# A fused attention and FFN kernel on one Trainium2 core: the last 128-token tile's output in two PSUM tiles, one for each half of the columns

## The chip, the core and the metric

The kernel runs on one core of one Trainium2 chip. The metric is the device time of one execution in microseconds (us); the median of three runs is used, and the profile is of one further execution. The engines are named as the profile names them: PE is the matrix engine (PEld its weight loads), DVE the vector engine, ACT the scalar engine, POOL the general one, SP the engine that issues most DMAs. A name with a q, SPq or ACTq, is the queue of instructions of that engine.

## The reference, cut to what matters

```python
a = exp(phi - max(phi, 2));  a = a / (sum(a, 2) + 1e-09)          # 8 batches, 8 heads, 576 tokens, 32 memories
k_m = einsum('bhsm,bhsd->bhmd', a, k);  v_m = einsum('bhsm,bhsd->bhmd', a, v)
attn = softmax(q @ k_m.T / sqrt(64))                              # per head, 576 x 32
x = (attn @ v_m), heads side by side                              # 4608 tokens x 512
h = x @ w_in                                                      # 512 -> 2048
out = maximum(0.01 * h, h) @ w_out                                # 2048 -> 512, float32
```

The change touches only the last product, `g @ w_out`, for the last 128 of the 4608 tokens, and the way from its result to DRAM.

## The kernel before, in words

The order of the work on every engine is written out by hand: two long strings, OPENING and LATER, name steps one after the other, and each step's function issues its instructions to the engines when its name comes up. No scheduler changes that order. On each engine the instructions run in the order of the strings, and an instruction waits until what it needs has been done elsewhere.

Tokens are worked in groups. Groups 0 to 2 (384 tokens each) cover batches 0 and 1, groups 3 to 16 cover the other six batches with 256 tokens each, except group 16, the last, which has 128. The hidden width of 2048 is cut into four quarters (j), and a quarter into four slices of 128 (i). Steps of the late groups are numbered by k = 4 * (group - 3) + j, so that 52 to 55 are the four quarters of group 16. For each of them the LATER string has:

- `p` (up_late, L1215): the up products of one slice into a PSUM tile `ph`, on PE (L1229);
- `v` (leaky_late): scale and leaky ReLU from `ph` to SBUF, on ACT (L1245);
- `c` and `l`: the values split into a high and a low half-precision part, ACT (L1270) and DVE (L1274);
- `d`: the down products. For the groups of 256 tokens they are down_late (L1297, 256 columns wide, with sums of weights prepared beforehand). For group 16 they are down_tile (L1324 to L1335): per slice three matmuls (high by high, high by low, low by high) of 128 x 128 by 128 x 512 that all add up in one PSUM tile `po`, 4 quarters x 4 slices x 3 = 48 in all;
- `x` and `z` for the groups of 256 tokens: the parts added up on DVE, the result scaled on ACT (L1321) and stored.

The string ends with `end`, that is `store(16, 0, ..., last=True)` (L1166): ACT scales the left 256 columns of `po` into SBUF (`obs`, L1170), DVE the right 256 (L1171), and `send` (L1156) then stores the 128 tokens in four DMAs of 32 tokens, each 32 rows of 512 floats (64 KB). Two are issued by SP and two by ACT (L1164). Every other store of the kernel goes through SP. A store's rows lie 18 rows apart in DRAM, because token 18 * x + j of a batch stands in column 32 * j + x of the tile: one store is one j and its 32 values of x.

At the end of the program SP waits for the stores that are still on their way (L1480), and a few synchronisation instructions on all engines close the span.

Of the kernel before, what the change touches and what calls it, by code (L numbers as in the profile page):

```python
# [9 lines left out]
F32 = mybir.dt.float32  # L10
# [6 lines left out]
AF = mybir.ActivationFunctionType  # L17
# [155 lines left out]
c51.0 s51 p52.0 p52.1 v52.0 d50.0 v52.1 l51.0 c51.1 d50.1 d50.2 c52.0 l51.1 p52.2 d50.3 v52.2 l52.0  # L173
d50.4 p52.3 d50.5 v52.3 d50.6 c52.1 l52.1 p53.0 p53.1 v53.0 d51.0 v53.1 d51.1 x15.p c53.0 d51.2
l53.0 p53.2 x15.0 d51.3 v53.2 d51.4 x15.1 p53.3 x15.2 d51.5 v53.3 d51.6 c53.1 p54.0 x15.3 v54.0
l53.1 d52.0 z15.0 z15.1 p54.1 d52.1 v54.1 p54.2 c54.0 d52.2 v54.2 l54.0 p54.3 d52.3 v54.3 p55.0
c54.1 d53.0 l54.1 v55.0 p55.1 d53.1 v55.1 p55.2 c55.0 d53.2 l55.0 v55.2 p55.3 d53.3 v55.3 d54.0
c55.1 l55.1 d54.1 d54.2 d54.3 d55.0 d55.1 d55.2 d55.3 end
"""


# [1 line left out]
def kernel(  # L183
# [41 lines left out]
    nc = tc.nc  # L225
    B, H, S, D = q.shape
    M = phi.shape[3]
    F = w_in.shape[1]
    E = w_out.shape[1]
    P = 128  # L230
# [8 lines left out]
    NQ = 4  # L239
    FQ = F // NQ  # L240
    NC = H * D // P
    NF = FQ // P
# [6 lines left out]
    EH = E // 2  # L249
    JT = S // 32  # L250
    JA = JT - 2
    G2 = 3
# [11 lines left out]
    ps_o = ctx.enter_context(tc.tile_pool(name="ps_o", bufs=3, space=PSUM))  # L264
# [13 lines left out]
    wi_s, wo_s = (  # L278
        [t.bitcast(F16).rearrange("p (i x) -> p i x", i=2) for t in ts[:NQ]] for ts in (wi, wo)
    )  # L280
# [26 lines left out]
    obs = const.tile([P, 3 * E], F32, name="obs")  # L307
# [777 lines left out]
    def blocks(G):  # L1085

        return [(G // 3 * 2 + x // NB, x % NB) for x in range(G % 3 * 2, G % 3 * 2 + 2)]
# [49 lines left out]
    def columns(G, t):  # L1137

        if G < G2:
            for x in range(t * P, (t + 1) * P, 32):  # L1140
                b, tb = blocks(G)[x // SB]
                yield b, tb * SB + x % SB
        else:
            x0 = 2 * S + (G - G2) * 2 * HT + t * P
            for x in range(x0, x0 + P, 32):
                yield x // S, x % S

    def row_scale(G, t):
        bs = [b for b, _ in columns(G, t)]
        if G == 0:  # L1150
            return 1.0 / WT
        if bs[0] == bs[-1]:
            return osc[:, bs[0]:bs[0] + 1]
        return osc_t[:, bs[0] // 2:bs[0] // 2 + 1]

    def send(G, t, ob, last=False):  # L1156
        for y, (b, x) in enumerate(columns(G, t)):
            rows, eng = out[b * S:(b + 1) * S, :], nc.scalar if last and y % 2 else nc.sync
            if b < FB:
                rows = rows.rearrange("(tb x j) e -> tb j x e", tb=NB, j=NJ)  # L1160
                rows = rows[x // SB, x % SB // 32]
            else:
                rows = rows.rearrange("(x j) e -> j x e", j=JT)[x // 32]
            eng.dma_start(rows, ob[32 * y:32 * y + 32])  # L1164

    def store(G, t, po, last=False):  # L1166
        so = row_scale(G, t)
        ob = obs[:, t * E:(t + 1) * E]
        if last:
            nc.scalar.activation(ob[:, 0:EH], po[:, 0:EH], AF.Copy, scale=so)  # L1170
            nc.vector.tensor_scalar_mul(ob[:, EH:], po[:, EH:], so)  # L1171
        else:
            nc.scalar.activation(ob, po, AF.Copy, scale=so)
        send(G, t, ob, last)

    pos = {}

# [30 lines left out]
    def whole(G):  # L1208

        return 2 * S + (G - G2 + 1) * 2 * HT <= B * S  # L1210
# [4 lines left out]
    def up_late(k, i):  # L1215

        G, j = G2 + k // NQ, k % NQ
        if not banks:
            banks["p1"], banks["ph"] = [ps_h.tile([P, E], F32, name="ph") for _ in range(2)]
        ph = banks["ph"][:, i % 2 * EH:(i % 2 + 1) * EH]  # L1220
        fs = slice(i * P, (i + 1) * P)
        for b, c0, n, t0 in parts(G):
            w, a = w16(b, j), a_columns(b)
            seq = [
                (halves(w, g)[:, x, fs], a[:, y, g, c0:c0 + n])
                for g in range(NG) for x, y in ((0, 0), (1, 0), (0, 1))
            ]
            for m, (lhs, rhs) in enumerate(seq):
                nc.tensor.matmul(  # L1229
                    ph[:, t0:t0 + n], lhs, rhs, start=(m == 0), stop=(m == len(seq) - 1)  # L1230
                )

    def leaky_late(k, i):
        G, j = G2 + k // NQ, k % NQ
        ph = banks["ph"][:, i % 2 * EH:(i % 2 + 1) * EH]
        st = late.setdefault(k, {})
        if "gf" not in st:
            st["gf"] = wi[NQ][:, k % 2 * 1024:(k % 2 + 1) * 1024]
            st["g"] = at(TMP + k % 3 * 7168, 7168).bitcast(F16)
        if whole(G):  # L1240
            dst = st["gf"].rearrange("p (s u x) -> p s u x", s=4, u=2)
            dst, ph = dst[:, i % 2 * 2:i % 2 * 2 + 2, i // 2], ph.rearrange("p (t x) -> p t x", t=2)
        else:
            dst, ph = st["gf"][:, i * HT:(i + 1) * HT], ph[:, 0:HT]
        nc.scalar.activation(dst, ph, AF.Prelu, scale=g_sc2[:, j:j + 1], alpha=SLOPE)  # L1245
# [13 lines left out]
    def add_g(k):  # L1259
        gf = late[k]["gf"].rearrange("p (s x) -> p s x", s=4)  # L1260
        gt = operands(k)[1]
        for x, y, z, op in (
            (0, gf[:, 0], gf[:, 2], ALU.add), (3, gf[:, 1], gf[:, 0], ALU.subtract),
            (1, gf[:, 1], gt[:, 0], ALU.subtract), (2, gf[:, 3], gt[:, 1], ALU.add),
        ):
            nc.vector.tensor_tensor(gt[:, x], y, z, op)  # L1266

    def hi_g(k, h):
        src, dst = operands(k)[h], operands(k)[2 + h]
        nc.scalar.copy(dst[:, 0], src)  # L1270

    def lo_g(k, h):
        src, dst = operands(k)[h], operands(k)[2 + h]
        nc.vector.tensor_tensor(dst[:, 1], src, dst[:, 0], ALU.subtract)  # L1274
# [44 lines left out]
    def finish(G, t):  # L1319
        ob = obs[:, (1 - t) * E:(2 - t) * E]  # L1320
        nc.scalar.activation(ob, ob, AF.Copy, scale=row_scale(G, t))  # L1321
        send(G, t, ob)

    def down_tile(k, i):  # L1324

        G, j = G2 + k // NQ, k % NQ
        if (j, i) == (0, 0):
            pos[G] = [ps_o.tile([P, E], F32, name="po")]
        g = late[k]["g"][:, 0:2 * FQ].rearrange("p (i s x) -> p i s x", i=2, s=NF)
        for m, (x, y) in enumerate(((0, 0), (0, 1), (1, 0))):  # L1330
            nc.tensor.matmul(  # L1331
                pos[G][0], g[:, x, i], wo_s[j][:, y, i * E:(i + 1) * E],
                start=(j == 0 and i == 0 and m == 0),
                stop=(j == NQ - 1 and i == NF - 1 and m == 2),
            )  # L1335
# [5 lines left out]
    steps = {}  # L1341
# [76 lines left out]
    for G in range(G2):  # L1418
        for t in range(NT):
            steps[f"Z{G}.{t}"] = lambda G=G, t=t: store(G, t, pos[G][t])  # L1420
# [4 lines left out]
    for m in range(nq):  # L1425
        for i in range(NF):
            steps[f"p{m}.{i}"] = lambda k=m, i=i: up_late(k, i)
            steps[f"v{m}.{i}"] = lambda k=m, i=i: leaky_late(k, i)
        steps[f"s{m}"] = lambda k=m: add_g(k)
        for h in range(2):  # L1430
            steps[f"c{m}.{h}"] = lambda k=m, h=h: hi_g(k, h)
            steps[f"l{m}.{h}"] = lambda k=m, h=h: lo_g(k, h)
        for n in range(7 if whole(G2 + m // NQ) else NF):
            steps[f"d{m}.{n}"] = lambda k=m, n=n: (
                down_late if whole(G2 + k // NQ) else down_tile
            )(k, n)
    for G in range(G2, G2 + NG2):
        for n in ("1", 0, 1, 2, 3):
            steps[f"x{G}.{'p' if n == '1' else n}"] = lambda G=G, n=n: combine(G, n)
        for t in range(2):  # L1440
            steps[f"z{G}.{t}"] = lambda G=G, t=t: finish(G, t)
    G = G2 + NG2 - 1
    steps["end"] = lambda: store(G, 0, pos[G][0], last=True)
    for b in range(B):
        steps[f"os{b}"] = lambda b=b: out_scale(b)

# [38 lines left out]
```

## Time and profile before

| what | value |
|---|---|
| time, median of 3 runs | 655.1 us (654.94 to 655.29) |
| span of the profiled execution | 652.3 us, 2.8 us less than that median |
| PE busy | 637.4 us, 98% of the span |
| DVE, ACT, POOL busy | 516.2, 392.7, 29.1 us |
| TensorE clock granted, mean | 0.989 |
| stores of the output | 142 issued by SP, 2 by ACT, 64 KB each |

The span runs from the first instruction of the program to the last. The rest of the measured time lies before and after it, and no view shows it. A row of the chain of waits gives the start in us, the length in us and the work; "issue" is time in which the engine waited for nothing that the profile shows. A row of the timeline has the start, the length, the engine, the line, the instruction, what it writes and reads, the number of instructions that are merged in it, and in brackets the idle time before it and who ended it. In the view of the DMA the first two lines cut the window into 40 equal slices: busy share of the 16 DMA engines in tenths (their mean), and GB/s. A row of the stretches gives the window, its length, the busy time of PE, PEld, DVE, ACT and POOL with the number of instructions, then the granted clock, the mean busy share of the 16 DMA engines (it can pass 1, since packets of one engine overlap) and GB/s.

### The profile page before, as it was taken

The numbers are of one execution on the slowest core, as the hardware profiler recorded it, in microseconds if no ns is written. First come the engines' busy times: TensorE is split into PE (matmuls) and PEld (weight loads), VectorE is DVE, ScalarE is ACT, GpSimd is POOL, SyncE is SP. The second block draws the span as 40 slices with busy tenths as digits, with TensorE's granted clock in tenths as the row PEclk, the third lists the DMA queues.
The fourth block names the chain that finished last, engine by engine and source line by source line (L and its number), as shares of the span: only waits on it lengthen the run. The fifth ranks groups of instructions, "written<-read, shape, count | busy, mean of one in ns | idle before, by whom it ended". The sixth has DMA issues, their size and how long they took to land.

```text
span 652.3 us, 17093 instructions
## 1 busy us (share of the span) xinstructions
PE 637.4 (98%) x7256; PEld 478.2 (73%) x7256; DVE 516.2 (79%) x863; ACT 392.7 (60%) x671; POOL 29.1 (4%) x37
## 2 busy tenths in 40 slices
PE   7899999999999999999999999999999999999997
PEld 3445545675545778888888888887878888889883
DVE  5875789998997899899969975889887897575641
ACT  2797878765463555557546565655675566565543
POOL 0010031000001001001000010000010001000000
PEclk8799999999999999999999999999999999999999
DMA  9989823105601654431154011064104110010102
GB/s 281 404 312 326 261 68 92 39 11 100 195 2 32 135 156 64 115 112 38 28 122 147 1 33 43 18 127 146 34 18 84 21 28 23 13 30 5 34 2 50
DMA packets 85309, 61.16 MB, mean 94 GB/s; under 512 B 61936, under 2 KB 68336, under 8 KB 85232
## 3 DMA queue, kind: packets, MB, share of 16 engines
q1 hardware_dynamic: 85136, 59.94, 32.8%
q8 instruction: 57, 0.93, 0.6%
q10 hardware_dynamic: 96, 0.13, 0.1%
q14 instruction: 20, 0.16, 0.1%
HBM read 50.59 MB, written 9.45 MB: 92 GB/s over the span
## 4 chain that ended last, share of the span: by engine, by line
PE 97%; DVE 1%; ACT 1%; issue 0%; POOL 0%; ACTq 0%; DVEq 0%; POOLq 0%
PE po L1297 32%; PE ph L1229 22%; PE po L1186 16%; PE ph L1114 8%; PE ph L1297 5%; PE pa L1020 4%; PE pa L698 3%; PE pa L1387 2%; PE po L1331 1%; PE pa L861 1%; PE pa L887 1%; ACT wi L1245 1%; PE pa L344 0%; PE po L698 0%; PE pa L777 0%
## 5 line engine op out<-in xcount | busy, mean ns | idle before, releaser
L1297 PEld LDWEIGHTS <-arena 128*128 128x128 f16 x2184 | 209.8, 98 | 32.0 <-issue 8.8
L1245 ACT ACTIVATE wi<-ph,g_sc 128x256 f32<-128x256 f32 (+1 forms) x224 | 99.3, 466 | 164.5 <-PE ph L1229 156.2
L1229 PE MATMUL ph<-a,w_mem 128*128 128x256 f16 (+3 forms) x1440 | 145.3, 246 | 2.9 <-ACT wi L1245 2.9
L1229 PEld LDWEIGHTS <-w_mem 128*128 128x128 f16 x1440 | 114.6, 98 | 17.8 <-issue 6.3
L1297 PE MATMUL po<-arena 128*128 128x256 f16 x936 | 122.1, 273 | 0.0
L1297 PE MATMUL po<-wo,arena 128*128 128x256 f16 x936 | 122.1, 273 | 0.0
L1186 PE MATMUL po<-wo,arena 128*128 128x512 f16 (+1 forms) x384 | 110.4, 434 | 0.0
L1274 DVE TENSOR_TENSOR arena<-arena 128x1024 f16<-128x1024 f32 x52 | 63.5, 1222 | 22.4 <-ACT arena L1270 22.4
L1274 DVE TENSOR_TENSOR arena<-wi,arena 128x768 f16<-128x768 f32 (+1 forms) x60 | 54.7, 911 | 10.1 <-ACT arena L1270 10.1
L1266 DVE TENSOR_TENSOR arena<-wi 128x256 f32<-128x256 f32 x104 | 40.4, 430 | 25.6 <-ACT wi L1245 25.1
L1270 ACT CAST arena<-arena 128x1024 f16<-128x1024 f32 x52 | 54.5, 1047 | 8.1 <-DVE arena L1266 8.0
L1114 PE MATMUL ph<-a,w_mem 128*128 128x192 f16 (+2 forms) x304 | 51.9, 317 | 0.7 <-DVE a L953 0.7
L1186 PEld LDWEIGHTS <-arena 128*128 128x128 f16 x288 | 27.8, 98 | 29.9 <-issue 0.6
L1270 ACT CAST arena<-wi 128x768 f16<-128x768 f32 (+1 forms) x60 | 46.6, 777 | 1.5
L1266 DVE TENSOR_TENSOR arena<-wi,arena 128x256 f32<-128x256 f32 x104 | 45.7, 440 | 1.8
L1297 PE MATMUL ph<-wo,arena 128*128 128x256 f16 x312 | 42.6, 273 | 0.0
L985 POOL TENSOR_TENSOR a<-t,a 128x1024 f16<-128x1024 f32 (+2 forms) x16 | 21.5, 1360 | 432.9 <-ACT a L980 432.9
L1186 PEld LDWEIGHTS po<-wo,arena 128*128 128x128 f32 x96 | 17.7, 190 | 21.4 <-issue 19.0
L1020 PE MATMUL pa<-wi,vT 64*32 64x512 f16 (+1 forms) x704 | 28.9, 420 | 0.4 <-ACT vT L805 0.4
L1121 ACT ACTIVATE arena<-ph,g_sc 128x384 f32<-128x384 f32 x32 | 18.5, 582 | 15.6 <-PE ph L1114 15.3
L1053 ACT ACTIVATE w_mem<-pa 128x512 f16<-128x512 f32 x40 | 22.7, 596 | 8.4 <-PE pa L1020 7.4
L1114 PEld LDWEIGHTS <-w_mem 128*128 128x128 f16 x240 | 20.7, 98 | 9.7 <-issue 3.6
(216 smaller groups left out, 757.8 us busy)
## 6 DMA issues: line engine op xcount, KB each, us to landing
out_dram<-obs SPq DMA_DIRECT2D x142, 64.0 KB, 1.7
arena<-in_k_dram SPq DMA_DIRECT2D x28, 288.0 KB, 4.5
arena<-in_v_dram SPq DMA_DIRECT2D x28, 288.0 KB, 5.3
arena<-in_q_dram SPq DMA_DIRECT2D x96, 72.0 KB, 2.8
arena<-in_moe_w_in_dram SPq DMA_DIRECT2D x12, 512.0 KB, 9.3
arena<-in_moe_w_out_dram SPq DMA_DIRECT2D x8, 768.0 KB, 6.8
arena<-in_phi_dram SPq DMA_DIRECT2D x7, 576.0 KB, 5.3
arena<-in_q_dram SPq DMA_DIRECT2D x4, 576.0 KB, 8.7
```

The costliest lines, as they stand in the source:

```text
L698: nc.tensor.matmul(var["pk"][g][hh * M:(hh + 1) * M, cs], ld["phi"][rows, hh, j, :], ld["kv", hh][rows, kinds[0]:kinds[-1] + 1, j, :], sta ...
L985: nc.gpsimd.tensor_tensor(piece(lo, tb), piece(t2, tb), piece(hi, tb), ALU.subtract)
L1020: nc.tensor.matmul(pf[g][cols, :], lhs, rhs, start=(n == 0), stop=(n == len(passes) - 1), tile_position=(g * D, hh * M),)
L1053: nc.scalar.activation(tiles(halves(w16(b, j), g)[:, 0]), w(g), AF.Copy, scale=ws)
L1114: nc.tensor.matmul(ph[:, t0:t0 + n * SB], lhs, rhs, start=(m == 0), stop=(m == len(seq) - 1))
L1186: nc.tensor.matmul(po, lhs, rhs, start=(f == 0 and m == 0), stop=(f == NQ * NF - 1 and m == len(seq) - 1),)
L1229: nc.tensor.matmul(ph[:, t0:t0 + n], lhs, rhs, start=(m == 0), stop=(m == len(seq) - 1))
L1245: nc.scalar.activation(dst, ph, AF.Prelu, scale=g_sc2[:, j:j + 1], alpha=SLOPE)
L1266: nc.vector.tensor_tensor(gt[:, x], y, z, op)
L1270: nc.scalar.copy(dst[:, 0], src)
L1274: nc.vector.tensor_tensor(dst[:, 1], src, dst[:, 0], ALU.subtract)
L1297: nc.tensor.matmul(acc, g[:, x, s, u], rhs, start=(h == 0 and j == 0 and u == 0 and m == 0), stop=(j == NQ - 1 and u == 1 and m == 2), ski ...
```

## The change

Group 16's output is accumulated in two PSUM tiles instead of one, for the columns 0 to 255 and 256 to 511. The step `d52.0` now does the left half of slice 0 and a new step `d52.4` the right half, and so on for 16 slices; each of the 48 matmuls of 512 columns becomes two of 256. The string places the two halves of a slice side by side, except in the last quarter, where the four left slices stand before `end.0` and the four right ones behind it:

```diff
-c55.1 l55.1 d54.1 d54.2 d54.3 d55.0 d55.1 d55.2 d55.3 end
+c55.1 l55.1 d54.1 d54.5 d54.2 d54.6 d54.3 d54.7 d55.0 d55.1 d55.2 d55.3 end.0 d55.4 d55.5 d55.6 d55.7 end.1
```

The step `end.0` scales the left half on ACT, `end.1` the right half on DVE, and each half is stored by two DMAs, one issued by SP and one by ACT. `store` and `send` lose their argument `last`; what they do for all other groups stays. The core of the diff:

```diff
+    def store_half(G, h, po):
+
+        ob, cs = obs[:, h * E:h * E + EH], slice(h * EH, (h + 1) * EH)
+        if h:
+            nc.vector.tensor_scalar_mul(ob, po[:, 0:EH], row_scale(G, 0))
         else:
-            nc.scalar.activation(ob, po, AF.Copy, scale=so)
-        send(G, t, ob, last)
+            nc.scalar.activation(ob, po[:, 0:EH], AF.Copy, scale=row_scale(G, 0))
+        rows = out.rearrange("(b x j) e -> b j x e", b=B, j=JT)
+        (b, x0), n = next(columns(G, 0)), P // 32
+        for y in range(0, n, n // 2):
+            eng = nc.sync if y == 0 else nc.scalar
+            src = ob[32 * y:32 * (y + n // 2)]
+            eng.dma_start(rows[b, x0 // 32 + y:x0 // 32 + y + n // 2, :, cs], src)
...
-            pos[G] = [ps_o.tile([P, E], F32, name="po")]
+            pos[G] = [ps_o.tile([P, E], F32, name="po") for _ in range(2)]
+        h, i = i // NF, i % NF
         g = late[k]["g"][:, 0:2 * FQ].rearrange("p (i s x) -> p i s x", i=2, s=NF)
         for m, (x, y) in enumerate(((0, 0), (0, 1), (1, 0))):
             nc.tensor.matmul(
-                pos[G][0], g[:, x, i], wo_s[j][:, y, i * E:(i + 1) * E],
+                pos[G][h][:, 0:EH], g[:, x, i],
+                wo_s[j][:, y, i * E + h * EH:i * E + (h + 1) * EH],
...
-    steps["end"] = lambda: store(G, 0, pos[G][0], last=True)
+    for h in range(2):
+        steps[f"end.{h}"] = lambda h=h: store_half(G, h, pos[G][h])
```

A store now takes 64 tokens and 256 columns: two values of j, 32 of x, and rows of 256 floats. It is 64 KB as before, but 64 rows of 1 KB where a store was 32 rows of 2 KB, and its pattern in DRAM has the outermost size 2 (the two j), then 32, then 256.

What the two strings make of ACT's instructions at the very end of the program (names of semaphores behind "waits": PE_49 is PE's, DVE_49 DVE's, Activation_49 ACT's own, the DMAHW ones are those of DMAs). Before:

```order
L1245 ACTIVATE wi_89<-ph,g_sc_101 128x128 [waits DVE_49,PE_49]
L1245 ACTIVATE wi_89<-ph,g_sc_101 128x128 [waits PE_49]
L1270 CAST arena<-wi_89 128x256 [waits Activation_49]
L1170 ACTIVATE obs<-po,osc 128x256 [waits DMAHW2_49,DMAHW1_49,DMAHW7_49,DMAHW0_49,PE_49]
L1164 DMA out_dram<-obs 32x512 [waits DMAHW3_49,DVE_49]
L1164 DMA out_dram<-obs 32x512 [waits DMAHW6_49]
```

And now, in the numbering of the changed file:

```order
L1254 ACTIVATE wi_89<-ph,g_sc_101 128x128 [waits DVE_49,PE_49]
L1254 ACTIVATE wi_89<-ph,g_sc_101 128x128 [waits PE_49]
L1279 CAST arena<-wi_89 128x256 [waits Activation_49]
L1177 ACTIVATE obs<-po,osc 128x256 [waits DMAHW2_49,DMAHW1_49,DMAHW7_49,DMAHW0_49,PE_49]
L1183 DMA out_dram<-obs 2x32x256 [waits DMAHW3_49,Activation_49]
L1183 DMA out_dram<-obs 2x32x256 [waits DMAHW5_49,DVE_49]
```

ACT's first store no longer waits for DVE but for ACT's own scaling of the left half; only the second waits for DVE. The shape of the stores has changed from 32x512 to 2x32x256.

The end of SP's program, as the difference of the two (the long row of 42 like stores is shortened by two, and two of the new form follow):

```order
 L1164 DMA out_dram<-obs 32x512 x8
 L575 DMA arena<-in_q_dram 32x18x32 x16
-L1164 DMA out_dram<-obs 32x512 x42
-L1480 UNCONDITIONAL_BRANCH
+L1164 DMA out_dram<-obs 32x512 x40
+L1183 DMA out_dram<-obs 2x32x256 x2
+L1492 UNCONDITIONAL_BRANCH
```

SP issues as many stores as before, two of them in the new form. DVE's last instruction, the scaling of the right half, waited for ACT and now waits for PE instead, since the two halves stand in two PSUM tiles.

More of the change, by code (lines that the diff above doesn't have):

```diff
@@ L175 @@
 l53.0 p53.2 x15.0 d51.3 v53.2 d51.4 x15.1 p53.3 x15.2 d51.5 v53.3 d51.6 c53.1 p54.0 x15.3 v54.0
-l53.1 d52.0 z15.0 z15.1 p54.1 d52.1 v54.1 p54.2 c54.0 d52.2 v54.2 l54.0 p54.3 d52.3 v54.3 p55.0
-c54.1 d53.0 l54.1 v55.0 p55.1 d53.1 v55.1 p55.2 c55.0 d53.2 l55.0 v55.2 p55.3 d53.3 v55.3 d54.0
-c55.1 l55.1 d54.1 d54.2 d54.3 d55.0 d55.1 d55.2 d55.3 end
+l53.1 d52.0 d52.4 z15.0 z15.1 p54.1 d52.1 d52.5 v54.1 p54.2 c54.0 d52.2 d52.6 v54.2 l54.0 p54.3 d52.3 d52.7 v54.3 p55.0
+c54.1 d53.0 d53.4 l54.1 v55.0 p55.1 d53.1 d53.5 v55.1 p55.2 c55.0 d53.2 d53.6 l55.0 v55.2 p55.3 d53.3 d53.7 v55.3 d54.0 d54.4
+c55.1 l55.1 d54.1 d54.5 d54.2 d54.6 d54.3 d54.7 d55.0 d55.1 d55.2 d55.3 end.0 d55.4 d55.5 d55.6 d55.7 end.1
 """
@@ L1154, in row_scale, with send @@
         return osc_t[:, bs[0] // 2:bs[0] // 2 + 1]
-    def send(G, t, ob, last=False):
+    def send(G, t, ob):
         for y, (b, x) in enumerate(columns(G, t)):
-            rows, eng = out[b * S:(b + 1) * S, :], nc.scalar if last and y % 2 else nc.sync
+            rows = out[b * S:(b + 1) * S, :]
             if b < FB:
@@ L1163, in send, with store @@
                 rows = rows.rearrange("(x j) e -> j x e", j=JT)[x // 32]
-            eng.dma_start(rows, ob[32 * y:32 * y + 32])
-    def store(G, t, po, last=False):
-        so = row_scale(G, t)
+            nc.sync.dma_start(rows, ob[32 * y:32 * y + 32])
+    def store(G, t, po):
         ob = obs[:, t * E:(t + 1) * E]
-        if last:
-            nc.scalar.activation(ob[:, 0:EH], po[:, 0:EH], AF.Copy, scale=so)
-            nc.vector.tensor_scalar_mul(ob[:, EH:], po[:, EH:], so)
-        else:
-            nc.scalar.activation(ob, po, AF.Copy, scale=so)
-        send(G, t, ob, last)
+        nc.scalar.activation(ob, po, AF.Copy, scale=row_scale(G, t))
+        send(G, t, ob)
+    def store_half(G, h, po):
+        ob, cs = obs[:, h * E:h * E + EH], slice(h * EH, (h + 1) * EH)
+        if h:
+            nc.vector.tensor_scalar_mul(ob, po[:, 0:EH], row_scale(G, 0))
+        else:
+            nc.scalar.activation(ob, po[:, 0:EH], AF.Copy, scale=row_scale(G, 0))
[5 more added lines that the diff above has]
+            eng.dma_start(rows[b, x0 // 32 + y:x0 // 32 + y + n // 2, :, cs], src)
     pos = {}
@@ L1432 @@
             steps[f"l{m}.{h}"] = lambda k=m, h=h: lo_g(k, h)
-        for n in range(7 if whole(G2 + m // NQ) else NF):
+        for n in range(7 if whole(G2 + m // NQ) else 2 * NF):
             steps[f"d{m}.{n}"] = lambda k=m, n=n: (
```

## The prediction

> **What bounds the kernel now.** I read the page first, then the chain of waits at the end of the span, then the timeline, SP's waits and the DMA behind the last matmul.
>
> ```profile
> span 652.3 us, 17093 instructions
> ...
> PE 637.4 (98%) x7256; PEld 478.2 (73%) x7256; DVE 516.2 (79%) x863; ACT 392.7 (60%) x671; POOL 29.1 (4%) x37
> ...
> PE 97%; DVE 1%; ACT 1%; issue 0%; POOL 0%; ACTq 0%; DVEq 0%; POOLq 0%
> ```
>
> PE is the bound: 97% of the chain is its matmuls. Whatever the change adds to PE before its last matmul is paid in full. Only the last 4 us of the span are no PE time, and there the change works. The chain of waits from 641 us:
>
> ```profile
> 641.20 0.65 PE po L1331 x3
> 641.85 0.34 PE ph L1229 x6
> 642.18 5.84 PE po L1331 x27
> 648.03 0.02 issue
> 648.05 0.48 ACT obs L1170
> 648.53 0.03 issue
> 648.56 0.48 DVE obs L1171
> ```
>
> The 27 last matmuls end at 648.03; ACT scales the left half, and DVE the right half only when ACT is done. That is one after the other, 0.51 us more than if both ran at once. What follows is in the timeline:
>
> ```profile
> 649.07 0.78 SPq L1164 DMA_DIRECT2D out_dram<-obs  x2
> 649.08 0.86 ACTq L1164 DMA_DIRECT2D out_dram<-obs  x2
> ```
>
> SP's own waits in that stretch:
>
> ```profile
> SPq L1480 <- DMA out_dram<-obs: 1.4, 2, 1.2
> ```
>
> Each queue issues two stores, some 0.4 us apiece, so the last ones start at 649.07 + 0.39 = 649.46 and 649.08 + 0.43 = 649.51. SP then waits for stores until little before the end at 652.3. The end of the span is thus the landing of the last store plus a fixed rest. The DMA in the window 646 to 653, 0.175 us a slice:
>
> ```profile
> DMA  0000000000000000000000779999200000000000
> GB/s 0 0 0 0 0 0 0 0 0 0 0 0 0 0 0 0 0 0 0 0 0 0 187 164 234 234 340 281 59 0 0 0 0 0 0 0 0 0 0 0
> DMA packets 192, 0.26 MB, mean 37 GB/s; under 512 B 64, under 2 KB 64, under 8 KB 192
> ...
> q10 hardware_dynamic: 96, 0.13, 8.3%
> q1 hardware_dynamic: 96, 0.13, 6.5%
> issues: line engine op xcount, KB each, median us to landing
> out_dram<-obs SPq DMA_DIRECT2D x2, 64.0 KB, 1.7
> out_dram<-obs ACTq DMA_DIRECT2D x2, 64.0 KB, 2.0
> ```
>
> 22 slices are empty, so data starts at 646 + 22 x 0.175 = 649.85, 0.8 us behind the first issue. The last slice with data ends at 646 + 29 x 0.175 = 651.07. From there to 652.33 lie 1.26 us: completion, SP's wait, closing. I carry these 1.26 us over.
>
> **The change part by part.** *PE.* 48 matmuls of 512 columns become 96 of 256. The first cost 5.84 / 27 = 0.2163 us each. The second form, half precision with a weight load each, is the daily bread of L1297, for instance here:
>
> ```profile
> 629.77 1.31 PE po L1297 x12
> ```
>
> That is 0.1092 us each, 0.2184 a pair, 0.0021 more than one wide one; 48 x 0.0021 = 0.10 us, all of it on the path. A bound below that is nothing, since no row shows a pair of narrow matmuls faster than a wide one; above it, the rows of L1297 show none slower. The doubled weight loads are hidden under the matmul before, as in L1297; if that cover were gone each pair would cost more, and L1297 would show it. So PE ends at 648.13, and its last left-half matmul 12 x 0.109 = 1.31 us earlier, at 646.82.
>
> *Left half.* ACT starts 0.02 later and takes 0.48, then 0.03 to the issue: both queues issue their first store at 646.84 + 0.48 + 0.03 = 647.35, where the first store went out at 649.07. Nothing is queued behind on SP but the second store, on ACT neither; ACT's scaling was its last work. *Right half.* DVE no longer waits for ACT: it starts at 648.15, ends at 648.63, and the second stores are issued at 648.66. So the last store starts 649.51 - 648.66 = 0.85 us earlier than before. If a store then took as long as it did, that would be the gain.
>
> *The stores themselves.* This is the term that decides, and no row of before shows a store of this form. What the rows show is how a store is cut up: the two of ACT's queue left 96 packets, of which 64 are their 2 x 32 rows and 32 are small, 16 to a store (in all, 64 small ones for four stores). A store is dealt out in 16 equal shares of its outermost size, 2 whole rows and a closing packet to each share, and the 16 engines take one each. The stretch of those stores and a stretch of loads from the first stage:
>
> ```profile
> 649.80:650.90 1.10, 0.00 (x0) 0.00 (x0) 0.00 (x0) 0.00 (x0) 0.00 (x0) 1.00 0.90 229
> 24.00:28.00 4.00, 3.09 (x156) 1.98 (x162) 2.82 (x7) 3.71 (x6) 0.87 (x2) 1.00 1.01 412
> ```
>
> A mean of 0.90 over 16 engines means that practically all of them took part. By the code every DMA of this kernel has an outermost size that 16 divides (32, 64, 96 or 128). The new store's is 2: it can't be dealt out in 16 equal shares of that, only in two. I take it that it runs on two engines, 32 rows of 1 KB on each, and that both queues use the same two, as both use the same 16 now. Then all 256 KB of the last tile go through two engines, 128 KB or 128 packets of 1 KB on each.
>
> The price of it: at full load an engine moves 412 / 16 / 1.01 = 25.5 GB/s, 40 ns for 1 KB, 128 x 40 = 5.1 us. That row is for longer packets. Packets of 1 KB are seen in the kernel's loads of r1k, 64 rows of 1 KB each. First their issue in the timeline:
>
> ```profile
> 116.71 1.15 SPq L620 DMA_DIRECT2D r1k<-d_mx  x2
> ```
>
> And the DMA of the window 116 to 120, 0.1 us a slice:
>
> ```profile
> DMA  2000000000000000000022222233322321000000
> ...
> DMA packets 193, 0.14 MB, mean 35 GB/s; under 512 B 62, under 2 KB 190, under 8 KB 193
> ...
> q1 hardware_dynamic: 193, 0.14, 10.6%
> ```
>
> 10.6% of 16 x 4 us are 6.8 us for 193 - 62 = 131 packets with data, 52 ns each, 128 x 52 = 6.7 us. I take 44 ns, nearer to the first row since the queue is always full here: 128 x 44 = 5.6 us. From above there is the stretch of the four stores, 229 / 16 / 0.90 = 15.9 GB/s, 64 ns, 8.2 us; I take it for an end of the range alone, because two packets that overlap on an engine are counted twice there. The start: 0.8 us from issue to data for the stores of before; for the r1k loads, whose issues are longer too (1.15 us for two, 0.78 for SP's two stores), 116.0 + 20 x 0.1 - 116.71 = 1.3 us. I take 1.1.
>
> The sum: issue 647.35 + 1.1 = 648.45 first data; the right half's stores are ready at 648.66 + 1.1 = 649.76, long before the left half is through (648.45 + 2.8 = 651.25), so they wait behind it and the two engines never idle; 648.45 + 5.6 = 654.05 last data; + 1.26 = 655.31. Against 652.33 that is +3.0 us. The time outside the span is unchanged, so 655.1 + 3.0 = 658.1. The ends: 0.8 and 5.1 give 647.35 + 0.8 + 5.1 + 1.26 = 654.51, +2.2; 1.3 and 8.2 give 658.11, +5.8.
>
> The Trainium skill states this rule outright: its page "DMA: Bandwidth & Descriptors", section "Why a DMA increments its semaphore by 16 and not by 1", says that a DMA issued by SP or ACT runs on the largest number of engines, up to 16, that divides the outermost size above 1 of both its patterns, and on the lowest-numbered ones. By that rule these stores run on the same two engines, which speaks against this change; the trace agrees as far as it goes (16 small packets to a store of outer size 32), and no run so far shows a size below 16.
>
> **The rivals.** *Sixteen engines after all.* The SBUF side of the new store has 64 rows, 4 to an engine, and a division by it would leave nothing slow. Then the issue at 648.66, 1.1 us to data, and half of the data that took 1.22 us before, 0.6 us: 650.36 + 1.26 = 651.62, 0.7 us less, 654.4. With 0.8 it is 654.1; with the 1.3 us of the general loads 654.6. All of that is within 0.2% of before, 1.3 us, about what a measurement here can tell from no change. For it speaks that no row shows a narrow store, against it that the DRAM side has only 2 to deal. I give it 0.13, of which 0.02 for a gain that passes 1.3 us (issue and completion shorter at once).
>
> *Two engines for each queue, but not the same two.* Then an engine has 32 packets of each half: left 648.45 + 32 x 0.044 = 649.86, right 1.41 more, 651.27, + 1.26 = 652.53, +0.2, 655.3. The trace speaks against it as far as all engines serve both queues in the window above. The same page of the Trainium skill, section "Issuing engines are not separate DMA queues", has it that all queues run on the same engines; the 0.90 agrees. I give it 0.05.
>
> *The left half does not go early* (the change doesn't do what it says): a wait that holds ACT until PE's very end. Then all data starts at 648.66 + 1.1 and lasts 5.6: 655.36 + 1.26 = 656.62, +4.3, 659.4. Against it: ACT's first store waits for ACT alone in the new order, and the stores that used the same SBUF columns were issued long before. 0.02.
>
> **How the numbers follow.** The forecast, both halves through the same two engines, has 0.80: 658.1 us. Its range runs from +2.2, less the 0.35 us by which the runs of before differ, 656.9, to +5.8, 660.9. With the rival of the late left half, which falls inside, it holds 0.82 and leaves the other two out. Chances: faster 0.02, the same 0.11 + 0.05 = 0.16, slower 0.80 + 0.02 = 0.82.
>
> **What the profile after would show.** Right: the 54 last matmuls at 0.109 us, PE's end near 648.1; the left half's stores issued near 647.35, before PE's end; DVE's scaling released by PE and not by ACT; the last issue near 648.7. Behind it, some 5.6 us in which the DMA's mean busy share is near 2/16 (0.125, or up to twice that where packets overlap) and 23 GB/s an engine, some 46 in all; on ACT's queue 128 data packets and 2 small ones to a store, 132, not 160; a landing of 5 us and more for the last stores, and SP's last wait as long. Wrong would be: 16 small packets to a store and a share near 0.9, which is the first rival; a share near 4/16 for 3 us, the second; or a PE that ends more than 0.3 us later, which would mean that the narrow matmuls have a price that L1297 does not show.

## The result, and the profile after

The changed kernel takes 658.89 us (median of 6 runs, 657.74 to 660.96), the one before 655.02 us (6 runs, 653.04 to 655.29). The medians differ by 3.9 us. The ratio is 1.0074, 95% interval 1.0058 to 1.009, which is 3.8 to 5.9 us of the time before: slower. The time lies in the forecast range, 0.8 us above the forecast value of 658.1. Of the twelve executions of the first experiment below two took 1680 and 2495 us, for a reason that no run shows; they count in its median of 654.49 us and not in its ratio.

The profiled execution has a span of 656.7 us, 4.4 more than that of before. The chain of waits at its end, in the numbering of the changed file:

```profile
641.49 0.66 PE po L1341 x6
642.15 0.34 PE ph L1238 x6
642.48 5.91 PE po L1341 x54
648.39 0.03 issue
648.42 0.48 DVE obs L1175
```

PE ends at 648.39, 0.36 us later than before. Of that the narrow matmuls make 0.07 in the last stretch (54 in 5.91 where 27 took 5.84) and 0.01 in each group before it (six in 0.66 where three took 0.65). The rest was there before the last stretch; the same kernel's executions differ by more. DVE is released by PE, no longer by ACT. From the start of this scaling at 648.42 it is 8.3 us to the end of the span; before, it was 4.3 us from the start of ACT's at 648.05. The timeline and SP's waits show what fills them:

```profile
647.11 0.47 ACT L1177 ACTIVATE obs<-po,osc 128x256 f32<-128x256 f32 x1 [3.78 <-PE po L1341]
647.61 1.86 SPq L1183 DMA_DIRECT2D out_dram<-obs  x2
647.61 1.98 ACTq L1183 DMA_DIRECT2D out_dram<-obs  x2
648.42 0.48 DVE L1175 TENSOR_SCALAR obs<-po,osc 128x256 f32<-128x256 f32 x1 [4.63 <-PE po L1341]
```

```profile
SPq L1492 <- DMA out_dram<-obs: 6.2, 2, 3.6
```

The left half's stores do go out before PE ends, at 647.61. But SP waits 6.2 us for stores at the end, where it waited 1.4. The DMA in the window 647 to 657, 0.25 us a slice:

```profile
DMA  0000000111111011111111111111111110000000
GB/s 0 0 0 0 0 0 0 16 12 29 41 33 25 25 16 37 41 45 49 45 49 45 49 45 49 49 49 49 49 45 49 49 41 16 0 0 0 0 0 0
DMA packets 264, 0.26 MB, mean 26 GB/s; under 512 B 8, under 2 KB 264, under 8 KB 264
...
q1 hardware_dynamic: 132, 0.13, 4.9%
q10 hardware_dynamic: 132, 0.13, 3.7%
```

Eight small packets for four stores, two to a store, where before had sixteen to a store. The mean share of the 16 engines shows as 0 or 1 tenth in every slice, and no slice passes 49 GB/s, where the stores of before reached 340. The data runs from 648.85 to 655.45, 6.6 us, where it took 1.2. Two stretches of it, from the first data to about ACT's first, and from there to the last:

```profile
648.85:651.05 2.20, 0.00 (x0) 0.00 (x0) 0.05 (x1) 0.00 (x0) 0.00 (x0) 1.00 0.13 27
651.05:655.45 4.40, 0.00 (x0) 0.00 (x0) 0.00 (x0) 0.00 (x0) 0.00 (x0) 0.53 0.13 46
```

Both have the share of two engines of sixteen, 0.125. But in the first 2.2 us they moved only 27 GB/s, then 46, that is 23 GB/s an engine or 44 ns for 1 KB. By the share the two engines were not idle there: a share of 0.13 over 2.2 us and 58 packets makes 0.13 x 16 x 2.2 / 58 = 79 ns for a packet, where the second stretch has 44. In the first stretch only SP's queue had data at all (the DMA of the window 648.8 to 651.05 names no other); ACT's, issued at the same 647.61, came 3.4 us behind its issue:

```profile
DMA packets 58, 0.06 MB, mean 26 GB/s; under 512 B 0, under 2 KB 58, under 8 KB 58
...
q1 hardware_dynamic: 58, 0.06, 12.6%
```

Cut finer, the first stretch has three parts, a slow start, the full pace for 0.3 us, and then a second slow part:

```profile
648.85:649.37 0.52, 0.00 (x0) 0.00 (x0) 0.05 (x1) 0.00 (x0) 0.00 (x0) 1.00 0.12 14
649.37:649.67 0.30, 0.00 (x0) 0.00 (x0) 0.00 (x0) 0.00 (x0) 0.00 (x0) 1.00 0.13 48
649.67:651.05 1.38, 0.00 (x0) 0.00 (x0) 0.00 (x0) 0.00 (x0) 0.00 (x0) 1.00 0.13 27
```

### The profile page after: what moved, and what is told of

Same layout as the page of the kernel before. It is cut to its first block, busy times and chain, and to the rows that moved or that the text cites. A ratio compares the mean times of both kernels' runs of the same rounds, so it can differ in the third digit from the quotient of the medians.

```text
span 656.7 us, 17191 instructions
## 1 busy us (share of the span) xinstructions
PE 634.5 (97%) x7304; PEld 480.5 (73%) x7304; DVE 516.1 (79%) x863; ACT 391.8 (60%) x671; POOL 29.1 (4%) x37
## 4 chain that ended last, share of the span: by engine, by line
PE 93%; DMA 4%; ACT 1%; issue 0%; SPq 0%; DVE 0%; ACTq 0%
PE po L1306 31%; PE ph L1238 22%; PE po L1195 16%; PE ph L1114 8%; PE ph L1306 5%; PE pa L1020 4%; PE pa L698 3%; DMA arena<-in_moe_w_in_dram 2%; DMA arena<-in_moe_w_out_dram 1%; PE po L1341 1%; PE pa L861 1%; DMA wo<-in_k_dram 1%; ACT wi L1254 1%; PE pa L887 0%; PE pa L344 0%
```

## The experiments

Theory A is the forecast's: a store whose outermost size in DRAM is 2 is dealt to two engines, and that is the whole loss. Its rivals: B, rows of 1 KB are slow in themselves; C, the narrow matmuls and the split tile cost it; D, the general form of such a store (three sizes in its pattern where a store of before has two) is slow whatever its engines.

The times of single executions differ by some microseconds from one to the next, so each run is also read by its *tail*: from the start of the first scaling that waits for PE's last matmul (in the chain, the row behind PE's last one and its "issue") to the end of the span. A tail is that of one profiled execution, and the span is known to 0.1 us. "Before" in the last column are the runs of the kernel before on the same chip in the same job.

| run | span less start of the scaling = tail, us | small packets a store | time, us (median) | ratio to before, 95% interval |
|---|---|---|---|---|
| before | 652.3 - 648.05 = 4.3 | 16 | 655.02 | |
| the change | 656.7 - 648.42 = 8.3 | 2 | 658.89 | 1.0074 (1.0058 to 1.009), before 655.02 |
| e1, stores of 32 rows | 651.3 - 647.62 = 3.7 | 16 | 654.49 | 0.9983 (0.9967 to 0.9999), before 654.8 |
| e2, wide tile, narrow stores | 659.8 - 648.89 = 10.9 | 2 | 661.33 | 1.0089 (1.0069 to 1.0109), before 654.8 |
| e3, split tile only | 651.3 - 647.48 = 3.8 | 16 | 654.8 | 0.999 (0.9976 to 1.0005), before 654.8 |
| e4, outermost size 4 | 652.0 - 646.84 = 5.2 | 4 | 655.36 | 1.0016 (0.9996 to 1.0036), before 654.8 |
| e5, narrow stores all by SP | 656.9 - 648.47 = 8.4 | 2 | 659.55 | 1.0063 (1.0034 to 1.0092), before 654.94 |
| e6, left half narrow only | 653.4 - 647.42 = 6.0 | 2 and 16 | 656.67 | 1.0026 (1.0007 to 1.0046), before 654.94 |
| e7, as e2, by SP alone | 659.6 - 649.65 = 10.0 | 2 | 661.49 (one run) | before 654.94 |
| e8, one narrow store alone | 650.8 - 647.22 = 3.6 | 2 | 652.75 (one run) | before 656.0 (one run) |
| e9, right half narrow only | 658.7 - 652.14 = 6.6 | 16 and 2 | 660.62 (one run) | before 656.0 (one run) |

**e1: the change with stores of 32 rows.**

```diff
-        for y in range(0, n, n // 2):
-            eng = nc.sync if y == 0 else nc.scalar
-            src = ob[32 * y:32 * (y + n // 2)]
-            eng.dma_start(rows[b, x0 // 32 + y:x0 // 32 + y + n // 2, :, cs], src)
+        for y in range(n):
+            eng = nc.scalar if y % 2 else nc.sync
+            eng.dma_start(rows[b, x0 // 32 + y, :, cs], ob[32 * y:32 * y + 32])
```

> The changed kernel, but each half is stored by four DMAs of 32 rows and 256 columns (SP two, ACT two) in place of two of 2 x 32 rows: the outermost size in DRAM is 32 again, the packets stay at 1 KB. Theory A (an outermost size of 2 leaves two engines): 16 small packets to a store, data of the last stores over in about 1 us, and from the last matmul to the end of the span 0.03 + 0.48 + 0.03 + 0.42 for the scaling and the two issues of a queue, then the 2.8 us that the last store of before took from its issue to the end: 3.8 us where before had 4.3 and the change 8.3. Time 0.4 us under before, within 0.2% of it. Rival B (rows of 1 KB are what is slow): still 7 to 8 us from the last matmul to the end, 3 to 4 us slower than before. Rival C (the narrow matmuls in two PSUM tiles cost it): also slower than before, with PE's last stretch longer.

Its chain's last row and its DMA in the window 647 to 651, 0.1 us a slice:

```profile
647.62 0.48 DVE obs L1175
```

```profile
DMA  0000004983258720000377605783000000000000
...
DMA packets 384, 0.26 MB, mean 66 GB/s; under 512 B 128, under 2 KB 384, under 8 KB 384
...
out_dram<-obs SPq DMA_DIRECT2D x4, 32.0 KB, 1.5
out_dram<-obs ACTq DMA_DIRECT2D x4, 32.0 KB, 1.7
```

128 small packets for eight stores, 16 each; the left half is through (slices 6 to 14) before the right half's data begins (slice 19), and the whole right half takes a microsecond. The tail is 3.7 us, 0.6 less than before and 4.6 less than the change, with the same 1 KB rows, the same split tile and the same order. B and C fall.

**e2: the kernel before with narrow stores.** The four stores at the end become two, `rows[b, x0 // 32 + y:x0 // 32 + y + n // 2]` with all 512 columns, by SP and ACT; everything else is as before.

> The kernel before, one PSUM tile, scaled as before, but the end is stored by two DMAs of 2 x 32 rows and 512 columns (SP one, ACT one) in place of four of 32 rows. Theory A: 2 small packets to a store, 64 packets of 2 KB on each of two engines at some 84 ns, 5.4 us, and from the last matmul to the end 1.02 + 1.25 + 5.4 + 1.3 = 9.0 us, 4.7 us slower than before. Rival B (1 KB rows): the rows are 2 KB, so no slower than before, rather 0.4 us faster by one issue less on each queue. Rival C (split tile): no slower than before.

```profile
DMA packets 132, 0.26 MB, mean 26 GB/s; under 512 B 4, under 2 KB 4, under 8 KB 132
...
q1 hardware_dynamic: 66, 0.13, 5.4%
q10 hardware_dynamic: 66, 0.13, 3.5%
```

The shape of the stores alone, with rows of 2 KB and an untouched PE, makes the kernel before slower by 6.5 us: the cause in the change is the shape. But A expected a tail of 9.0 and it was 10.9. The data took 7.29 us at 36 GB/s where 5.4 us were expected, so the engines did not run at the expected rate all the time:

```profile
651.16:658.45 7.29, 0.00 (x0) 0.00 (x0) 0.00 (x0) 0.00 (x0) 0.00 (x0) 0.50 0.12 36
```

**e3: the split tile only.** ACT scales early, but the four stores of 32 full rows go out after DVE, as before.

```diff
-        rows = out.rearrange("(b x j) e -> b j x e", b=B, j=JT)
...
+        for y, (b, x) in enumerate(columns(G, 0) if h else ()):
+            rows, eng = out[b * S:(b + 1) * S, :], nc.scalar if y % 2 else nc.sync
+            rows = rows.rearrange("(x j) e -> j x e", j=JT)[x // 32]
+            eng.dma_start(rows, obs[32 * y:32 * y + 32, 0:E])
```

> The two PSUM tiles and the narrow matmuls of the change in its order, ACT scales the left half early, but nothing is stored early: four DMAs of 32 full rows as before go out when DVE has done the right half. Theory A: DVE no longer waits for ACT, so the stores start 0.5 us earlier; PE pays 0.1 us: 3.8 us from the last matmul to the end, 0.4 us under before, the same as the stores of 32 rows by halves, since each queue still issues two stores behind DVE. Rival C (split tile costs it): 3 us or more slower than before.

The end of its chain:

```profile
641.55 5.91 PE po L1339 x54
647.46 0.03 issue
647.48 0.48 DVE obs L1175
```

DVE starts 0.02 behind PE's end, and the tail is 3.8 us. The split is worth 0.5 us of the tail, the serial scaling, as expected. Storing the left half early on top of it (e1) makes 0.1 more, a difference as small as the rounding of the spans. In both cases each queue has two stores behind DVE, and the second sets the end. In the time neither is clear: e1's interval ends just below 1, e3's holds it.

**e4: outermost size 4.** One DMA to a half, `rows[b, x0 // 32:x0 // 32 + n, :, cs]`, the left by SP, the right by ACT.

> The changed kernel, but each half is one DMA of 4 x 32 rows and 256 columns, the left half by SP, the right by ACT: outermost size 4. Theory A: 4 small packets to a store, 32 packets of 1 KB on each of four engines for each half; left data from 1.25 us behind its issue, right data from 0.5 + 1.25 = 1.8 us behind the last matmul, 1.4 to 2.4 us long, + 1.3: 4.5 to 5.4 us from the last matmul to the end, 0.3 to 1.2 us slower than before. Rival B (1 KB rows): still near 8 us. Rival D (the general form of a store is slow whatever its engines, by its issue and start): the same 8 us as the change.

Its stretches of the left and the right half's data, and its packets:

```profile
647.30:649.02 1.72, 0.00 (x0) 0.00 (x0) 0.03 (x1) 0.00 (x0) 0.00 (x0) 0.94 0.26 78
649.00:650.65 1.65, 0.00 (x0) 0.00 (x0) 0.00 (x0) 0.00 (x0) 0.00 (x0) 0.50 0.24 79
```

```profile
DMA packets 264, 0.26 MB, mean 66 GB/s; under 512 B 8, under 2 KB 264, under 8 KB 264
```

Two stores, eight small packets: four to a store, a share of 4/16, twice the mean rate of the change (0.26 MB in 6.6 us, 40 GB/s), and a tail of 5.2 us, between the expected 4.5 and 5.4. D falls: the form is as general as the change's. Besides the outermost size, the number of stores differs too, one of 128 KB to a half in place of two of 64; the count of small packets and the share go with the size. Sizes 2, 4 and 32 gave 2, 4 and 16 small packets. By the Trainium skill ("DMA: Bandwidth & Descriptors", section "Why a DMA increments its semaphore by 16 and not by 1") the number of engines is the largest up to 16 that divides the outermost size of both sides. These runs agree for the three sizes, with 64, 128 and 32 rows on the SBUF side.

**e5: all narrow stores by SP.** What stayed open was the first stretch at 27 GB/s. ACT's first data came 3.4 us after its issue there, so the two queues might hinder each other. The edit takes the choice of the engine away: `nc.sync.dma_start` for all four.

> The changed kernel, but SP issues all four narrow stores and ACT none. In the profile of the change the first 64 packets of the left half took 2.2 us, until ACT's first data came 3.4 us behind its issue, and only then did a packet of 1 KB pass every 42.5 ns on each of the two engines. Theory P (two queues that deal to the same two engines at the same moment hinder each other's start): with one queue the packets pass at 42.5 ns from the start, 128 x 42.5 = 5.4 us where the change took 6.6, and from the right half's scaling to the end 0.4 + 5.4 + 1.3 = 7.2 us where the change had 8.3; 3 us slower than before. Rival Q (a narrow store starts slowly by itself): again 6.6 us of data and 8.3 us.

```profile
648.90:652.73 3.83, 0.00 (x0) 0.00 (x0) 0.06 (x1) 0.00 (x0) 0.00 (x0) 0.91 0.13 34
652.73:655.70 2.97, 0.00 (x0) 0.00 (x0) 0.00 (x0) 0.00 (x0) 0.00 (x0) 0.50 0.12 44
```

One queue alone moved the left half at 34 GB/s and the right at 44, 6.8 us in all, and the tail is 8.4. Theory P, the two queues' clash, falls as the cause in the change, since it expected 7.2; the first half is slow with one queue too.

**e6: only the left half narrow.** The right half goes out as in e1.

> The changed kernel, but only the left half, which is stored while the right one is computed, goes out in the two narrow stores; the right half goes out in four stores of 32 rows. Theory A: the left half's 64 packets on each of two engines begin 0.4 us behind the start of the right half's scaling and last 2.7 us and what the slow start costs, 3.5 to 3.8 in all, so the end comes 0.4 + 3.7 + 1.3 = 5.4 us behind that start, 1.1 us more than before: the head start of 1.3 us doesn't hide a store on two engines. If the early half were hidden for nothing: 3.7 us, as with stores of 32 rows throughout.

The tail is 6.0 us, 2.3 more than e1's and 0.6 above the expected 5.4. So the head start of 1.3 us doesn't hide a store on two engines; the right half's stores, which took 1.5 and 1.7 us to land in e1, took 4.0 here, behind the left half:

```profile
out_dram<-obs SPq DMA_DIRECT2D x1, 64.0 KB
out_dram<-obs ACTq DMA_DIRECT2D x1, 64.0 KB
out_dram<-obs SPq DMA_DIRECT2D x2, 32.0 KB, 4.0
out_dram<-obs ACTq DMA_DIRECT2D x2, 32.0 KB, 4.0
```

**e7: e2 with both stores by SP.**

> The kernel before with one PSUM tile and two narrow stores of 2 x 32 full rows at the end, both by SP, where the earlier run had one by SP and one by ACT and took 10.95 us from ACT's scaling to the end. Theory P: 64 packets of 2 KB at 84 ns on each engine from the start, 5.4 us, so 1.0 + 1.25 + 5.4 + 1.3 = 9.0 us. Rival Q: 10.9 us again.

10.0 us lies between the two expectations: P's clash is not the whole of it, and Q's full slowness did not come back either. With wide rows the tail with one queue was about 1 us shorter than with two, in one profiled execution of each, so a part for the second queue is not excluded there. It decides nothing alone.

**e8: one narrow store alone.** The loop `for y in range(0, n, n // 2)` becomes `for y in range(0, 1 - h)`: only the first of the four stores is left, and three quarters of the last tile's output stay unwritten.

> The changed kernel with only the first of its four narrow stores (SP, left half, 64 tokens); the other three are left out, so three quarters of the last tile's output are never written. It asks why the first 64 packets take 2.0 to 2.4 us where 64 / 2 x 42.5 ns = 1.4 us would do. Theory R (the stores that are issued behind it, on either queue, hold it up): alone it runs at full rate but for its first few packets, 1.4 to 1.7 us of data, small packets at the end. Rival Q (a narrow store is slow at first by itself): 2.0 us or more again.

```profile
647.66:648.17 0.51, 0.00 (x0) 0.00 (x0) 0.04 (x1) 0.00 (x0) 0.00 (x0) 1.00 0.12 16
648.17:649.40 1.23, 0.00 (x0) 0.00 (x0) 0.00 (x0) 0.00 (x0) 0.00 (x0) 1.00 0.13 47
```

With nothing issued behind it the store is slow for 0.5 us, then runs at 47 GB/s: 1.74 us in all for 64 KB, where the same store of the change had brought 58 of its 64 packets through after 2.2 us. That is a little over the top of R's range and clear of Q's. The slow start is that of the change (14 GB/s in its first 0.52 us), but the second slow part of the change, 649.67 to 651.05, is missing here.

**e9: only the right half narrow.** The left half goes out as in e1, the right in the change's two stores.

> The changed kernel, but the left half goes out early in four stores of 32 rows, the right half in the two narrow stores of the change, one by SP and one by ACT. Theory R: the second narrow store is issued at the same moment as the first, so the first is held up as in the change: 64 packets on each engine in 3.5 to 3.8 us, and from the right half's scaling to the end 0.5 + 1.25 + 3.6 + 1.3 = 6.6 us, 2.3 us more than before. Rival T (only the first touch of the rows in DRAM is slow; the left half has touched the same rows): 0.5 + 1.25 + 2.7 + 1.3 = 5.8 us.

```profile
653.90:655.88 1.98, 0.00 (x0) 0.00 (x0) 0.00 (x0) 0.00 (x0) 0.00 (x0) 1.00 0.13 30
655.88:657.45 1.57, 0.00 (x0) 0.00 (x0) 0.00 (x0) 0.00 (x0) 0.00 (x0) 0.74 0.13 46
```

Its scaling in the chain:

```profile
652.14 0.48 DVE obs L1175
```

The tail is 6.6 us as R had it. The rows in DRAM had been touched by the left half, yet the first narrow store ran at 30 GB/s, the second at 46. T falls. So the first narrow store is slow when another is issued beside or behind it (the change, e5, e9) and only at its start when alone (e8, a single execution); the last ones run at the engines' pace. What holds its packets up no view here shows, and it stays open.

## Why the prediction was right

The mechanism was right step by step; one term was too small. The forecast rise of 3.0 us lies below the measured 3.8 to 5.9.

- *PE.* 0.10 us were forecast; the last 54 matmuls took 0.07 more than the 27 wide ones, and the groups before them 0.01 each. Right, and e1 and e3 show that nothing else came with the split.
- *The head start.* Left stores 0.78 us before PE's end were forecast (647.35 against 648.13), and were issued at 647.61 against 648.39, 0.78. DVE was released by PE. Right.
- *Two engines.* Two small packets to a store, 132 packets on ACT's queue, a share of 0.13, the same two engines for both queues (46 GB/s in all, and a share that never doubled). Right, and e4 shows that it is the outermost size. The first two rivals, sixteen engines and separate pairs, are out by the same rows; the third, a late left half, by the issue at 647.61.
- *The start.* 1.1 us from issue to data were taken between 0.8 and 1.3; it was 648.85 - 647.61 = 1.24.
- *The data.* This is the mis-sized term: 5.6 us were taken, with 44 ns for 1 KB "since the queue is always full here"; it was 6.6. The 44 ns hold from 651.05 on (46 GB/s on two engines). The first 2.2 us ran at 27 GB/s, a loss of some 0.9 us against 46: a narrow store is slow at its start, alone too (e8), and slow a second time with others behind it. By the share the two engines were not idle, as the forecast had it, but a packet took 79 ns there and not 44; a full queue was no ground for the lower price. The range had room for it by the row of 52 ns: 128 x 52 = 6.7.
- *The rest.* 1.26 us from the last data to the end were carried over; it was 656.7 - 655.45 = 1.25.

In sum the tail grew by 4.0 us, where the forecast's own figures give 7.2 - 4.3 = 2.9; start 0.1 and data 1.0 are the difference. The medians moved by 3.9 us.

The gain of the change is there too: 0.5 us of the tail by the scaling that no longer waits (e3); the early left half adds some 0.1 to it (e1), if anything. With stores of 32 rows it is 4.6 us better in the tail than as it was made, and no slower than before, with 654.49 against 654.8 us.

## What to carry to other kernels

Before two small stores are merged into one to save an issue, look at the outermost size of the pattern on both sides: here one issue on each queue was saved behind the last scaling, and 2 in place of 32 cost 4.6 us. In these runs the count of small packets in the view of the DMA, by the number of stores, went with the number of engines that the mean share shows: 2 with 0.13, 4 with 0.25, 16 with 0.90. And where the end of a kernel is the landing of the last store, count what each queue still has to issue behind the last scaling; storing a part early was worth some 0.1 us here (e1 against e3), where each queue had two stores to issue behind the last scaling in both.

## What the runs showed of the hardware that was not expected

- A narrow store of 64 KB has a slow start: alone (e8) its first 0.51 us passed at 16 GB/s and the rest at 47.
- With another narrow store issued beside or behind it the first one took longer, 27 GB/s for 2.2 us in the change and 30 GB/s for 1.98 us in e9, and 34 GB/s over the whole left half in e5 on one queue.
- Narrow stores took longer to issue, ACT's first one most of all. The instructions of the changed kernel's stores, with the least, median and longest duration in ns:

```profile
L1183 SPq DMA_DIRECT2D out_dram<-obs x2: 539/593/647, 647.6 to 648.9; - x2
L1183 ACTq DMA_DIRECT2D out_dram<-obs x2: 527/940/1354, 647.6 to 649.1; - x2
```

Where the four stores of before took some 0.4 us each, these take 0.53 to 1.35, so that two stores merged into one saved little issue, or none.
